# A decayed linear-attention stage inside a three-part kernel: order of two scans, one copy of the state, place of the small VectorE operations

## The chip, the core and the metric

One NeuronCore of a Trainium2 chip runs the whole program. The metric is the time of one execution in microseconds, as the median of several runs. A profile of one execution goes with it: its engines are PE (TensorE matmul) with PEld (its weight loads), DVE (VectorE), ACT (ScalarE), POOL (GpSimd) and SP (SyncE, which issues DMAs here).

## The reference

Three computations follow each other: an attention with a decaying state, a mixture of experts that picks one of eight experts for each token, and a dense maxout block. The change lies in the first, and in the part of the second that sorts tokens to experts while the first still runs.

```
B, H, S, D = 4, 8, 768, 48
for t in range(S):
    cur = einsum('bhd,bhe->bhde', u * k[t], v[t])
    y[t] = einsum('bhd,bhde->bhe', r[t], state + cur)
    state = w[t][..., None] * state + einsum('bhd,bhe->bhde', k[t], v[t])
x = y as 3072 tokens of 384
expert_idx = argmax(normalised x @ normalised emb.T / tau);  gate = softmax value of it
out[mask_e] = gate * (relu(x[mask_e] @ w1[e]) @ w2[e])
h = max(out @ a, out @ b, out @ c);  result = h @ w_out
```

## The kernel before

**Chunks.** The 768 steps of each of four batches are cut into six chunks of 128, so there are 24 chunks; chunk `g` has place `c = g % 6` in its batch. Heads go in pairs: head `2p` lies on partitions 0 to 47, head `2p+1` on partitions 64 to 111, and a tile of four pairs has 112 partitions. For each chunk two scans along time give cumulated decays: `gs` from the end backwards, `es` from the start forwards (it needs one value of `gs` per pair, through the reciprocal into `dE`). The keys times `gs` are `kS`, the receptances times `es` are `rt`. `gram` multiplies them into scores in two banks `A` (one per head of a pair), `causal` copies the scores below the diagonal into `AT`, whose diagonal POOL wrote before. `outputs` adds the state's product (`shat` with `rt`) and the product of `AT` with the values in bank `Y`; `tokens` turns the result into token rows. `kback`, `update` and `carry` bring the state to the next chunk. In `carry`, POOL multiplies the new state with the next chunk's decays twice: into `shat`, a block-diagonal copy that `outputs` uses as weights of 112 by 112, and into `Sm`, the copy that the next `carry` adds to.

**Order.** The order of instructions is written by hand in a loop over `i` from -2 to 23; each engine takes its instructions in that order. In iteration `i` the kernel handles `carry(i)`, `outputs(i)` and `tokens(i)`; `gram`, `kback`, `causal` and `update` of `g = i+1`; the bonus terms and the diagonal of `j = i+2`; the transposes, scans and products of `h = i+3`. So `rt` and `kS` made in one iteration are used by `gram` two iterations later. On PE an iteration is: `gram(g)`, transposes of w, `kback`, bonus sum, transposes of k, `outputs(i)`, bonus turn, transposes of r, `update`, `tokens(i)`. `kback` and `update` are left out for a batch's last chunk, the state's product for its first.

**Banks.** The transposes of w, k and r go around two banks `T`: w of the next chunk needs the bank that k of this chunk was in, which is free when `kS` is made. Six users go around three banks `M`, `tokens` and `update` among them; `logits` (`dot`) and `carry` (`S`) on DVE set them free. At the start `transpose` of w for chunk 1 takes the bank `T` in which the k of chunk 0 lies.

**Routing.** Sets of three chunks (two at the end) are routed while attention goes on. `route_expert` gives five small DVE operations, in the iterations `i` = 3, 6, 9 and so on; `route_rank` counts ranks on PE and `route_slot` gives twelve small DVE operations in `i` = 4, 7, 10, 13, 16, 19. They are put in a list, `fillers`. `fill()` issues the next one from the list; it stands between the larger DVE operations (after each masked copy, after each scan, after `kS`), and `fill(99)` issues what is left at the end of the iteration.

Of the kernel before, what the change touches and what calls it, by code (L numbers as in the profile page):

```python
# [7 lines left out]
F32 = mybir.dt.float32  # L8
F32R = mybir.dt.float32r
BF16 = mybir.dt.bfloat16  # L10
# [29 lines left out]
NOWHERE = 100000  # L40

# [5 lines left out]
class Block:  # L47
# [64 lines left out]
    def attention(self):  # L112
# [3 lines left out]
        with ExitStack() as es:  # L116
# [44 lines left out]
            shat = [cp.tile([112, NP, 112], F32, name=f"shat{i}") for i in range(2)]  # L161
# [11 lines left out]
            cum = cp.tile([P, E], BF16, name="cum")  # L173
# [59 lines left out]
            def setup2b():  # L233
# [6 lines left out]
                for q, o in ((0, 0), (1, 64)):  # L240
                    act.activation(out=sel[o:o + D, :, q * D:(q + 1) * D],
                                   in_=ident[o:o + D, o:o + D].unsqueeze(1).to_broadcast([D, NP, D]), func=AF.Copy)
                act.activation(out=sel[:, :, 96:104], in_=tp[:112, :32].rearrange("q (p e) -> q p e", p=NP), func=AF.Copy)
                act.activation(out=flat(self.enT), in_=tq[:, :24], func=AF.Copy)

            def setup4():
                pool.memset(one1, 1.0)
                for k in range(E):
                    for i in range(2):
                        pool.memset(caprow[:, i, k:k + 1], float(CAPS[i][k]))  # L250
                for t, m, base in ((w7, -1, E - 1), (pos, 1, 0)):
                    pool.iota(t, pattern=[[m, E]], base=base, channel_multiplier=0, allow_small_or_imprecise_dtypes=True)

            def setup3():
                for t in yT + shat:
                    pool.memset(t, 0.0)
                pool.memset(acc, 0.0)
                pool.memset(cum, 0.0)
                pool.memset(oneb, 1.0)
                pool.affine_select(out=tri, in_=oneb, pattern=[[1, P]], compare_op=ALU.is_gt, fill=0.0,  # L260
                                   base=0, channel_multiplier=-1)
                for t, pat, base, mul in ((w8, [[-1, E]], E, 0), (i128, [[1, P]], 0, 0),
                                          (i32, [[1, 32]], -32, 0), (tid, [[P, NG]], 0, 1)):
# [5 lines left out]
            def transpose(g, which):  # L269
# [3 lines left out]
                t = bank("T", 2)  # L273
# [45 lines left out]
            def scan(g):  # L319
# [9 lines left out]
                x["kS"] = wp.tile([112, 512], F32, tag="kS", name="kS", bufs=3)  # L329
                scaled = lambda: dve.tensor_tensor(out=x["kS"].rearrange("q (p t) -> q p t", p=NP),  # L330
                                                   in0=x["k"][:112].rearrange("q (p t) -> q p t", p=NP),
                                                   in1=gs[:, :, 1:], op=ALU.mult)
                if g > 0:
                    scaled()
                fill()
# [4 lines left out]
                if g == 0:  # L340
                    scaled()
# [45 lines left out]
            def carry(g):  # L387
# [9 lines left out]
                j = (g + 1) % 2  # L397
                decay = lambda o, n: pend[o:o + n, g + 1, :].unsqueeze(2).to_broadcast([n, NP, D])
# [43 lines left out]
            def fill(n=1):  # L442
# [7 lines left out]
            def route_expert(g0, n):  # L450

                sl = slice(g0, g0 + n)
                r = rt_[g0] = {}
                b8 = lambda z: z.unsqueeze(2).to_broadcast([P, n, E])
                w8b = w8.unsqueeze(1).to_broadcast([P, n, E])
                m, e8, r["mx"], r["oh"] = (small("m", [P, n]), small("e8", [P, n, E]), small("mx", [P, n]),
                                           small("oh", [P, n, E], BF16))
                ops = [lambda: dve.tensor_reduce(out=m, in_=dot[:, sl, :], axis=X, op=ALU.max)]
                if n == 1:
                    ops += [lambda: dve.scalar_tensor_tensor(out=e8[:, 0], in0=dot[:, g0, :], scalar=m, in1=w8,  # L460
                                                             op0=ALU.is_equal, op1=ALU.mult)]
                else:
                    ops += [lambda: dve.tensor_tensor(out=e8, in0=dot[:, sl, :], in1=b8(m), op=ALU.is_equal),
                            lambda: dve.tensor_tensor(out=e8, in0=e8, in1=w8b, op=ALU.mult)]
                ops += [lambda: dve.tensor_reduce(out=r["mx"], in_=e8, axis=X, op=ALU.max),
                        lambda: dve.tensor_tensor(out=r["oh"], in0=w8b, in1=b8(r["mx"]), op=ALU.is_equal)]
# [814 lines left out]
```

## Time and profile before

| | |
|---|---|
| median of 3 runs | 737.52 us (733.77 to 738.44) |
| the profiled execution | 733.96 us, span 732.2 us, mean granted clock 0.992 |
| attention loop | from about 13 to 187 us of the span |
| PE, DVE, POOL busy | 708.7, 428.2, 257.0 us |

The span is what the profile covers. The attention loop takes the first quarter; the experts follow up to about 419 us and the dense block up to about 711 us.

### The profile page before, as it was taken

To read this page: it belongs to the slowest core of one execution; us is meant where nothing else is said; L and a number is where in the kernel's file an instruction comes from. 1 tells how busy PE (TensorE), PEld (TensorE's weight loads), DVE (VectorE), ACT (ScalarE), POOL (GpSimd) and SP (SyncE) were. 2 spreads that over 40 slices of the span, in tenths; PEclk is the share of its full clock that TensorE was granted. 3 is DMA by queue.
4 is the path that set the end of the run, shared out by engine and by line. 5 is a ranking of instruction groups with operands and counts; after the bars stand their busy time and mean duration, and the time that the engine had idled before them with its cause. 6 is when DMAs were issued, how large, how long until landed. Compare 5 with 4: busy or idle time off the path is not lost.

```text
span 732.2 us, 13468 instructions
## 1 busy us (share of the span) xinstructions
PE 708.7 (97%) x4861; PEld 627.6 (86%) x4861; DVE 428.2 (58%) x938; ACT 306.8 (42%) x720; POOL 257.0 (35%) x271
## 2 busy tenths in 40 slices
PE   7999999999799999999999999999999999999994
PEld 4788888888789999999999988988988988889884
DVE  7889999998747986878788368431032031221110
ACT  4667666765445554555556322222121221221120
POOL 6857657476531401201100023343333333223122
PEclk9999999999999999999999999999999999999998
DMA  9997878753365537656554111000100100000001
GB/s 154 171 149 139 138 135 138 144 89 118 104 186 165 170 115 216 202 152 195 152 173 147 60 29 59 23 22 1 44 1 0 44 1 11 33 1 21 22 2 46
DMA packets 146444, 69.05 MB, mean 94 GB/s; under 512 B 104967, under 2 KB 140931, under 8 KB 146360
## 3 DMA queue, kind: packets, MB, share of 16 engines
q1 hardware_dynamic: 141752, 58.27, 35.1%
q0 software_dynamic: 4032, 9.74, 4.2%
q8 instruction: 42, 0.69, 0.4%
q14 instruction: 42, 0.34, 0.1%
q10 hardware_dynamic: 576, 0.01, 0.1%
HBM read 58.52 MB, written 9.48 MB: 93 GB/s over the span
## 4 chain that ended last, share of the span: by engine, by line
PE 85%; DVE 7%; issue 3%; DMA 2%; ACT 1%; POOL 1%; SPq 0%; POOLq 0%; DVEq 0%; ACTq 0%
PE psy L993 16%; PE psT L993 15%; PE psy L933 13%; PE psh L916 13%; PE psh L1017 9%; PE psT L275 4%; PE psA L356 3%; PE psM L426 3%; PE psY L417 3%; PE psY L410 2%; PE psM L384 1%; DMA out_dram<-raw,idx 1%; DVE es L337 1%; PE psM L294 1%; DVE gs L324 1%
## 5 line engine op out<-in xcount | busy, mean ns | idle before, releaser
L999 DVE TENSOR_TENSOR xg<-psT,xg 128x512 f32<-128x512 f32 x18 | 12.4, 690 | 112.8 <-PE psT L993 80.8
L827 DVE TENSOR_TENSOR lw<-raw,hw 128x384 fp32r<-128x384 f32 x120 | 62.3, 553 | 15.8 <-ACT hw L825 14.0
L825 ACT ACTIVATE hw<-raw 128x384 fp32r<-128x384 f32 x123 | 60.7, 524 | 17.7 <-ACT hw L825 10.2
L1007 POOL TENSOR_TENSOR lw<-xg,hw 128x512 fp32r<-128x512 f32 x24 | 31.5, 1311 | 100.4 <-ACT hw L1006 100.4
L841 POOL DMA_INDIRECT xg<-xs_d,idxs x25 | 26.8, 1073 | 111.0 <-PE psT L903 44.6
L1007 POOL TENSOR_TENSOR lh<-xg,hh 128x512 fp32r<-128x512 f32 x12 | 16.1, 1340 | 115.1 <-ACT hh L1006 115.1
L309 POOL TENSOR_SCALAR_AFFINE_SELECT AT<-c 128x1024 f32<-128x1024 f32 x24 | 38.9, 1619 | 49.0 <-ACT c L304 48.9
L1006 ACT ACTIVATE hw<-xg 128x512 fp32r<-128x512 f32 x24 | 15.2, 635 | 97.0 <-DVE xg L1000 97.0
L993 PE MATMUL psy<-yh,mh 128*128 128x512 f32 x162 | 46.7, 396 | 0.2 <-ACT ys L937 0.2
L993 PE MATMUL psy<-yl,mh 128*128 128x512 f32 x162 | 46.6, 395 | 0.0
L993 PE MATMUL psT<-yh,ml 128*128 128x512 f32 x162 | 46.6, 396 | 0.0
L993 PE MATMUL psy<-yh,ml 128*128 128x512 f32 x162 | 46.5, 396 | 0.0
L993 PE MATMUL psT<-yl,mh 128*128 128x512 f32 x162 | 46.5, 396 | 0.0
L993 PE MATMUL psT<-yh,mh 128*128 128x512 f32 x162 | 46.5, 395 | 0.0
L922 DVE SCALAR_TENSOR_TENSOR lh<-psh,hh 128x420 fp32r<-128x420 f32 (+6 forms) x56 | 31.4, 561 | 19.8 <-ACT hh L921 19.5
L916 PE MATMUL psh<-xh,hw 128*128 128x420 f32 (+7 forms) x177 | 42.0, 345 | 0.3 <-DVE lh L922 0.3
L916 PE MATMUL psh<-xh,lw 128*128 128x420 f32 (+7 forms) x183 | 42.0, 339 | 0.0
L1033 POOL DMA_INDIRECT out_dram<-raw,idx x24 | 23.7, 987 | 49.5 <-ACT raw L1023 32.5
L916 PE MATMUL psh<-xl,hw 128*128 128x420 f32 (+7 forms) x177 | 40.7, 337 | 0.0
L933 PE MATMUL psy<-hh,hw 128*128 128x420 f32 (+6 forms) x168 | 40.1, 344 | 0.0
L933 PE MATMUL psy<-lh,hw 128*128 128x420 f32 (+6 forms) x168 | 39.2, 341 | 0.0
L933 PE MATMUL psy<-hh,lw 128*128 128x420 f32 (+6 forms) x168 | 39.2, 341 | 0.0
(329 smaller groups left out, 1801.7 us busy)
## 6 DMA issues: line engine op xcount, KB each, us to landing
raw<-in_moe_w_dram SPq DMA_DIRECT2D x128, 192.0 KB
raw<-in_moe_w_dram SPq DMA_DIRECT2D x18, 384.0 KB
wb<-in_w_dram SPq DMA_DIRECT2D x24, 192.0 KB
kb<-in_k_dram SPq DMA_DIRECT2D x24, 192.0 KB
rb<-in_r_dram SPq DMA_DIRECT2D x24, 192.0 KB
vb<-in_v_dram SPq DMA_DIRECT2D x24, 192.0 KB
xs_d<-xt SPq DMA_DIRECT2D x24, 192.0 KB
raw<-in_moe_w_out_dram SPq DMA_DIRECT2D x6, 384.0 KB
```

The costliest lines, as they stand in the source:

```text
L275: pe.transpose(t[:112, p * P:(p + 1) * P], flat(src)[:, p * P:p * P + 112], ident)
L309: pool.affine_select(out=x["AT"].rearrange("s q p t -> s (q p) t"), in_=x["c"].rearrange("t q p -> t (q p)").unsqueeze(2).to_broadcast([P, ...
L825: self.act.activation(out=hi, in_=raw, func=AF.Copy)
L827: eng.tensor_tensor(out=lo, in0=raw, in1=hi.bitcast(F32), op=ALU.subtract)
L841: self.pool.indirect_dma_start(out=t[:n], out_offset=None, in_=self.xs_d[0:rows], in_offset=bass.IndirectOffsetOnAxis(ap=self.idxs[:n, 4 * ...
L916: self.pe.matmul(t[:, c0:cap], a[:, d, :], b[:, d, c0:], start=(n == 0), stop=(n == 8))
L922: self.dve.scalar_tensor_tensor(out=lo, in0=t[:, c0:cap], scalar=0.0, in1=hi.bitcast(F32), op0=ALU.max, op1=ALU.subtract)
L933: self.pe.matmul(self.yb[m][:, :cap], a[:, m, :], b, start=(f == 0 and n == 0), stop=(f == 7 and n == 2))
L993: self.pe.matmul(t, a[:, d, f * P:(f + 1) * P], b[:, d, :], start=(n == 0), stop=(n == 8))
L1007: self.pool.tensor_tensor(out=lo, in0=c2, in1=hi.bitcast(F32), op=ALU.subtract)
L1017: self.pe.matmul(t[:, :DM], a[:, c], b[:, f, :], start=(n == 0), stop=(n == 17))
L1033: self.pool.indirect_dma_start(out=self.out, out_offset=bass.IndirectOffsetOnAxis(ap=self.idx2[:, k:k + 1], axis=0), in_=o, in_offset=None ...
```

## The change

The state is kept once: POOL writes one tile `held` of 112 by 192, which is the weights of the state's product and the summand of the next `carry`. The state's product is written as eight products of 48 rows instead of four of 112. Both scans stand ahead of `kS` and `rt` for every chunk. In the loop up to `i` = 19 the small operations all stand behind the two masked copies; from `i` = 20 on `fill()` works as before. Transposes of w for chunk 1 take a bank `A`. Ranks are counted with wider products (nine become four for a set of three), in doubled numbers; the counting of a set is one reduction into the next set's tile instead of three additions; the list's slot needs one operation less, and `aa` has one tensor operand instead of two. Some constants are made by other small instructions.

```
-            shat = [cp.tile([112, NP, 112], F32, name=f"shat{i}") for i in range(2)]
+            held = [cp.tile([112, NP * D + 16], F32, name=f"held{i}") for i in range(2)]
...
+                dve.tensor_scalar(out=i32, in0=i32, scalar1=HALF + 0.5, scalar2=None, op0=ALU.add)
...
-                t = bank("T", 2)
+                t = bank("A" if (g, which) == (1, "w") else "T", 2)
...
                 fill()
-                x["kS"] = wp.tile([112, 512], F32, tag="kS", name="kS", bufs=3)
-                scaled = lambda: dve.tensor_tensor(out=x["kS"]..., in1=gs[:, :, 1:], op=ALU.mult)
-                if g > 0:
-                    scaled()
-                fill()
                 dve.tensor_tensor_scan(out=flat(es_), data0=wz[j][:, :-1], data1=flat(dE), ...)
                 x["es"] = es_
-                if g == 0:
-                    scaled()
+                fill()
+                x["kS"] = wp.tile([112, 512], F32, tag="kS", name="kS", bufs=3)
+                dve.tensor_tensor(out=x["kS"]..., in1=gs[:, :, 1:], op=ALU.mult)
                 fill()
...
-                for o in (0, 64):
-                    pool.tensor_tensor(out=shat[j][o:o + D, :, o:o + D], in0=sn[o:o + D], in1=decay(o, D), op=ALU.mult)
-                if c < CH - 2:
-                    state[b] = wp.tile([112, NP, D], F32, tag="Sm", name="Sm", bufs=1)
-                    pool.tensor_tensor(out=state[b], in0=sn, in1=decay(0, 112), op=ALU.mult)
+                hold = state[b] = held[(g + 1) % 2][:, :NP * D].rearrange("q (p e) -> q p e", p=NP)
+                pool.tensor_tensor(out=hold, in0=sn, in1=pend[:, g + 1, :].unsqueeze(2).to_broadcast([112, NP, D]),
+                                   op=ALU.mult)
...
                     for p in range(NP):
-                        pe.matmul(t[:112, p * P:(p + 1) * P], shat[j][:, p, :], x["rt"][:, p * P:(p + 1) * P],
-                                  start=(p == 0), stop=False)
+                        for o, m in ((0, 64), (64, D)):
+                            pe.matmul(t[o:o + m, p * P:(p + 1) * P], held[j][o:o + D, p * D:p * D + m],
+                                      x["rt"][o:o + D, p * P:(p + 1) * P], start=(p == 0), stop=False)
...
-            def fill(n=1):
+            def fill(n=None):
+                if n is None:
+                    n = len(spread)
...
-                for i in range(n):
-                    o = rk[:, i * E:(i + 1) * E]
-                    pe.matmul(o, oneb, cum, start=True, stop=False)
-                    for k in range(i):
-                        pe.matmul(o, oneb, r["oh"][:, k, :], start=False, stop=False)
-                    pe.matmul(o, tri, r["oh"][:, i, :], start=False, stop=True)
+                pe.matmul(o, twob, r["cum"].unsqueeze(1).to_broadcast([P, n, E]), start=True, stop=False)
+                for k in range(n - 1):
+                    pe.matmul(o[:, k + 1:], twob, r["oh"][:, k:k + 1].to_broadcast([P, n - 1 - k, E]), ...)
+                pe.matmul(o, tri, r["oh"], start=False, stop=True)
...
-                    return lambda: dve.tensor_tensor(out=cum, in0=cum, in1=r["oh"][:, i, :], op=ALU.add)
+                        dve.tensor_reduce(out=ohs[(r["set"] + 1) % 3][:, 0], in_=ohs[r["set"] % 3][:, :n + 1]..., op=ALU.add)
...
-                    lambda: dve.tensor_scalar(out=rq, in0=ri, scalar1=7, ..., op0=ALU.logical_shift_right),
-                    lambda: dve.tensor_scalar(out=rl, in0=ri, scalar1=4095 - 384, ..., op0=ALU.bitwise_and),
-                    lambda: dve.scalar_tensor_tensor(out=aa, in0=r["mx"], scalar=-4.0, in1=rq, op0=ALU.mult, op1=ALU.add),
+                    lambda: dve.tensor_scalar(out=rl, in0=ri, scalar1=1, scalar2=4095 - 384, ...),
+                    lambda: dve.tensor_scalar(out=aa, in0=ri, scalar1=2.0 ** -8, scalar2=HALF, op0=ALU.mult, op1=ALU.add),
...
+                    if i == NG - 4:
+                        spread.append(True)
...
                         causal(g)
+                    if not spread:
+                        fill(99)
...
-                    fill(99)
+                    if spread:
+                        fill(99)
```

## Rows read from the trace of the kernel before

**Rows 1.** The page: busy time by engine, and the chain that ended last.

```profile
PE 708.7 (97%) x4861; PEld 627.6 (86%) x4861; DVE 428.2 (58%) x938; ACT 306.8 (42%) x720; POOL 257.0 (35%) x271
...
PE 85%; DVE 7%; issue 3%; DMA 2%; ACT 1%; POOL 1%; SPq 0%; POOLq 0%; DVEq 0%; ACTq 0%
```

**Rows 2.** Busy time by stretch: length, PE, PEld, DVE, ACT, POOL, clock, DMA.

```profile
34.60:185.00 150.40, 148.30 (x1844) 126.66 (x1844) 136.19 (x325) 100.37 (x268) 96.92 (x115) 1.00 0.72 130
```

**Rows 3.** The chain, 85.0 to 92.3 us (i = 9): start, length, what.

```profile
85.03 1.09 PE psA L356 x16
86.12 0.58 PE psT L275 x4
...
88.02 0.88 PE psY L410 x8
88.90 1.01 PE psY L417 x16
...
90.17 0.44 PE psT L275 x4
...
91.20 1.07 PE psM L426 x8
```

**Rows 4.** DVE in order of time, i = 7: start, length, what.

```profile
70.75 0.75 DVE L362 COPY_PREDICATED AT<-msk,psA 128x512 f32<-128x512 int32 x1
...
72.69 1.22 DVE L324 TENSOR_TENSOR_SCAN gs<-wz,dG 112x516 f32<-112x516 f32 x1
...
76.16 0.69 DVE L348 TENSOR_TENSOR rt<-psT,es 112x512 f32<-112x512 f32 x1
...
77.00 1.20 DVE L505 SCALAR_TENSOR_TENSOR aa<-mx,rq 128x3 f32<-128x3 f32 x1
...
78.59 0.70 DVE L495 TENSOR_SCALAR pay<-i,aa,tid 128x32 fp32r<-128x32 f32 x3
...
79.31 0.34 DVE L396 TENSOR_TENSOR S<-Sm,psM 112x192 f32<-112x192 f32 x1
```

**Rows 5.** POOL in order of time, i = 7.

```profile
76.92 1.27 POOL L288 TENSOR_TENSOR z<-kT,rT 112x512 f32<-112x512 f32 x1
```

**Rows 6.** PE in order of time, i = 8: idle time before it and releaser in brackets.

```profile
79.54 0.43 PE L294 MATMUL psM<-z,uh 112*32 112x128 f32 x8 [0.47 <-DVE dot L437]
```

**Rows 7.** The chain, 49.0 to 55.6 us (i = 4, batch's last chunk in gram).

```profile
49.07 1.09 PE psA L356 x16
...
50.95 0.36 PE psM L294 x8
...
54.47 1.14 PE psM L426 x8
```

**Rows 8.** ACT in order of time, i = 4.

```profile
53.30 0.21 ACT L327 ACTIVATE pend<-gs 112x4 f32<-112x4 f32 x1 [0.72 <-DVE gs L324]
53.82 0.60 ACT L419 ACTIVATE yT<-psY 112x512 f32<-112x512 f32 x1 [0.31 <-PE psY L417]
```

**Rows 9.** DVE in order of time, i = 21: dependent small operations without a large one between.

```profile
174.66 0.15 DVE L500 TENSOR_TENSOR ro<-psM,oh 128x16 f32<-128x16 f32 x1
...
175.05 0.17 DVE L503 TENSOR_SCALAR rq<-ri 128x2 int32<-128x2 int32 x1
```

**Rows 10.** All engines in order of time, 8 to 18 us, chunks 0 and 1.

```profile
10.02 0.68 DVE L348 TENSOR_TENSOR rt<-psT,es 112x512 f32<-112x512 f32 x1
...
10.16 1.10 PE L275 MATMUL psT<-ident,wb 128*112 128x128 f32 x4 [2.04 <-DVE kS L330]
...
11.93 1.23 DVE L324 TENSOR_TENSOR_SCAN gs<-wz,dG 112x516 f32<-112x516 f32 x1 [1.23 <-ACT wz L277]
...
14.16 1.91 DVE L337 TENSOR_TENSOR_SCAN es<-wz,dE 112x516 f32<-112x516 f32 x1
...
14.96 2.17 POOL L288 TENSOR_TENSOR z<-kT,rT 112x512 f32<-112x512 f32 x1
...
17.19 0.42 PE L294 MATMUL psM<-z,uh 112*32 112x128 f32 x8 [1.38 <-POOL z L288]
```

More of the change, by code (lines that the diff above doesn't have):

```diff
@@ L40 @@
 NOWHERE = 100000
+HALF = 2.0 ** 23 - 0.5
 def flat(t):
@@ L172, in attention @@
             tri = cp.tile([P, P], BF16, name="tri")
-            cum = cp.tile([P, E], BF16, name="cum")
+            twob = cp.tile([P, P], BF16, name="twob")
+            ohs = [cp.tile([P, 4, E], BF16, name=f"ohs{i}") for i in range(3)]
             acc = cp.tile([P, 32], F32, name="acc")
@@ L250, in setup4 @@
                         pool.memset(caprow[:, i, k:k + 1], float(CAPS[i][k]))
-                for t, m, base in ((w7, -1, E - 1), (pos, 1, 0)):
-                    pool.iota(t, pattern=[[m, E]], base=base, channel_multiplier=0, allow_small_or_imprecise_dtypes=True)
+                pool.iota(pos, pattern=[[1, E]], base=0, channel_multiplier=0, allow_small_or_imprecise_dtypes=True)
+                dve.tensor_scalar(out=w7, in0=pos, scalar1=-32769.0, scalar2=E - 1 - 8192.0, op0=ALU.mult, op1=ALU.add)
             def setup3():
-                for t in yT + shat:
+                for t in yT + held:
                     pool.memset(t, 0.0)
                 pool.memset(acc, 0.0)
-                pool.memset(cum, 0.0)
                 pool.memset(oneb, 1.0)
-                pool.affine_select(out=tri, in_=oneb, pattern=[[1, P]], compare_op=ALU.is_gt, fill=0.0,
+                pool.memset(twob, 2.0)
+                pool.affine_select(out=tri, in_=twob, pattern=[[1, P]], compare_op=ALU.is_gt, fill=0.0,
                                    base=0, channel_multiplier=-1)
-                for t, pat, base, mul in ((w8, [[-1, E]], E, 0), (i128, [[1, P]], 0, 0),
-                                          (i32, [[1, 32]], -32, 0), (tid, [[P, NG]], 0, 1)):
+                pool.affine_select(out=tri, in_=tri, pattern=[[1, P]], compare_op=ALU.not_equal, fill=1.0,
+                                   base=0, channel_multiplier=-1)
+                for t, pat, base, mul in ((w8, [[-1, E]], E, 0), (i128, [[1, P]], 1024, 0), (ohs[0][:, 0], [[32, E]], 8, 0),
+                                          (i32, [[32, E], [1, 4]], 8, 0), (tid, [[P, NG]], 0, 1)):
                     pool.iota(t, pattern=pat, base=base, channel_multiplier=mul,
@@ L440, in attention @@
             rt_, fillers = {}, []
-            def fill(n=1):
+            spread = []
+            def fill(n=None):
+                if n is None:
+                    n = len(spread)
                 while fillers and n:
@@ L452, in route_expert @@
                 sl = slice(g0, g0 + n)
-                r = rt_[g0] = {}
+                k = len(rt_)
+                r = rt_[g0] = {"set": k}
+                r["cum"], r["oh"] = ohs[k % 3][:, 0], ohs[k % 3][:, 1:n + 1]
                 b8 = lambda z: z.unsqueeze(2).to_broadcast([P, n, E])
                 w8b = w8.unsqueeze(1).to_broadcast([P, n, E])
-                m, e8, r["mx"], r["oh"] = (small("m", [P, n]), small("e8", [P, n, E]), small("mx", [P, n]),
-                                           small("oh", [P, n, E], BF16))
+                m, e8, mx = small("m", [P, n]), small("e8", [P, n, E]), small("mx", [P, n])
                 ops = [lambda: dve.tensor_reduce(out=m, in_=dot[:, sl, :], axis=X, op=ALU.max)]
[L459 to L466, printed above, removed]
+                ops += [lambda: dve.tensor_tensor(out=e8, in0=dot[:, sl, :], in1=b8(m), op=ALU.is_equal),
+                        lambda: dve.tensor_tensor(out=e8, in0=e8, in1=w8b, op=ALU.mult),
+                        lambda: dve.tensor_reduce(out=mx, in_=e8, axis=X, op=ALU.max),
+                        lambda: dve.tensor_tensor(out=r["oh"], in0=w8b, in1=b8(mx), op=ALU.is_equal)]
                 return ops
@@ L488, in rank, with count @@
                         dve.tensor_reduce(out=ri, in_=ro, axis=X, op=ALU.add)
-                def count(i):
-                    return lambda: dve.tensor_tensor(out=cum, in0=cum, in1=r["oh"][:, i, :], op=ALU.add)
+                def count():
+                    with nc.allow_low_precision(reason="small integers"):
+                        dve.tensor_reduce(out=ohs[(r["set"] + 1) % 3][:, 0],
+                                          in_=ohs[r["set"] % 3][:, :n + 1].rearrange("p n e -> p e n"), axis=X, op=ALU.add)
                 def place(i):
@@ L496, in place @@
                                                      scalar2=tid[:, g:g + 1], op0=ALU.is_equal, op1=ALU.mult)
-                return ([count(i) for i in range(n)] if g0 + n < NG else []) + [
+                return ([count] if g0 + n < NG else []) + [
                     lambda: dve.tensor_tensor(out=ro, in0=r["rk"][:, :n * E].rearrange("q (n e) -> q n e", n=n),
@@ L543, in totals @@
                 tot = st["tot"] = bank("M", 3)
-                pe.matmul(tot[:1, :E], oneb[:, 0:1], cum, start=True, stop=False)
+                pe.matmul(tot[:1, :E], oneb[:, 0:1], rt_[g0]["cum"], start=True, stop=False)
                 for k in range(n):
@@ L564, in leader @@
                 tp = bank("T", 2)
-                pe.matmul(tp[:1, :E], oneb[:, 0:1], cum, start=True, stop=True)
+                pe.matmul(tp[:1, :E], oneb[:, 0:1], ohs[6 % 3][:, 0], start=True, stop=True)
                 return [
```

20 lines of the change are left out of this document (9 added, 11 removed).

## The prediction

> **What bounds the kernel now.** I read first the page's busy times and the chain that ended last [rows 1]: PE is busy 97% of the span and makes 85% of the chain, DVE 7%. So what an edit gives on DVE, ACT or POOL counts only where PE waits for it. Then busy time by stretch: in the attention loop's steady part, 34.6 to 185 us, PE is busy 148.30 of 150.40 us [rows 2]. It idles 2.1 us in all, and that is four waits of about half a microsecond (i = 8, 14, 20, 21), of which the first stands in [rows 6]. In the chain of an undisturbed iteration [rows 3] every step is a PE step; the iteration is as long as PE's instructions. The experts and the dense block behind the loop are PE's as well and not touched, so the sum is how much earlier or later the attention loop ends.
>
> One thing must be seen before costing DVE: `rt` and `kS` of an iteration are used by `gram` two iterations later. A later `rt` does not hold up the next `gram`. What holds PE up from DVE is a bank that is released late, or an ACT step queued behind a late scan.
>
> **A. The state's product.** Before, four products of 128 columns take 0.88 us, 0.22 each at line L410 [rows 3]. After, eight products, each 48 rows to half of the output partitions. The trace of before has no product that is halved both ways; the nearest rows are the eight products of `AT` with the values, halved by output partitions, 1.01 us for eight of 128 columns, and `gram`, halved by input rows, 1.09 us [rows 3]. Both show that two halves overlap: one after the other, eight at 0.22 would be 1.76. I also read a price for a change of form: the same four transposes take 0.58 us right behind `gram` and 0.44 behind another transpose [rows 3], and the new product follows transposes of full size and precedes the products with the values, so it pays that. I take 1.01, the nearest row: +0.13 us. Bounds: nothing (0.88; a gain is excluded because as many columns stream through each half as before) to 1.76 (+0.88). There are 20 chunks with a state; in three of them PE waits anyway (D), so 17 × 0.13 = **+2.2 us**, bounds 0 to +17.6.
>
> The halves of the new product write into one bank, at different partitions, while those of `gram` write into two banks. The Trainium skill, TensorEngine Tiling (Array Packing), section Restrictions and Gotchas, says: "Different row tiles cannot access same PSUM bank simultaneously". No row here shows such a case; by that rule the halves would come one after the other, which is the upper bound just given, and the sum would be some 15 us higher. It is the first rival below.
>
> **B. Ranks.** Nine products take 0.21 us: from the end of the transposes at 49.07 + 1.09 + 0.58 = 50.74 to 50.95 [rows 3, 7]. Four take about 0.1. Six sets in the loop, three of them in iterations of D: 3 × 0.11 = **-0.3 us**.
>
> **C. Small operations off the place behind `rt`.** In iteration 7, `rt` ends at 76.85, and then the rest of the list runs until `S` at 79.31 [rows 4]: 2.4 us, of which `aa` alone is 1.20, because it ends with POOL's `z` at 78.19 [rows 4, 5]. `S` releases a bank `M`, and PE waits 0.47 us for that [rows 6] (the trace names `dot`, the operation just before `S`). After, nothing stands between `rt` and `dot`, and the counting, in a tile of its own, needs no wait for PE. Then `rt` ends 8.0 us behind the begin of `gram` (1.2 to the copies, 1.3 for them, 1.8 for the small operations, see D, and 3.7 for scans and products: 72.69 to 76.85 less the small operations between [rows 4]) and `S` 0.4 later; PE wants the bank 9.5 us behind it, at 79.07 [rows 6]. Of the four waits one is at i = 21, behind the leader's small operations, which stay where they were; but DVE comes to them some 1.5 us earlier, so that it goes as well. **-2.1 us**; bounds -2.1 to -1.5 (the last stays).
>
> **D. What the small operations delay instead.** All of a set's operations now stand ahead of `gs`. Their length, n = 3: counting 0.1, two dependent steps 0.39 [rows 9], `rl` and `aa` 0.2, `ohb` 0.4 (78.20 to 78.59), `pay` 0.6 [rows 4]: about 1.8 us. On ACT the copy `pend` waits for `gs`, and queued behind it are `yT`, the turn of the bonus terms, `rT` and `xt`; `tokens` on PE waits for `yT`. In iteration 4, which has no `kback` and `update` to fill the time, `gram` begins at 49.07 and `tokens` at 54.47 [rows 7], `pend` at 53.30 and `yT` at 53.82 [rows 8]. After: copies from 49.07 + 1.2, two of them 1.3, small operations 1.8, `gs` 1.22 [rows 4], so `pend` at 54.6, `yT` 0.21 later, done 0.60 later at 55.4: `tokens` about 0.85 us late. Three iterations are like that (4, 10, 16): **+2.5 us**. In the others of the kind (7, 13, 19) `kback` and `update` put `tokens` 6.2 us behind the begin of `gram` [rows 3], and `yT` is ready 6.3 behind it: 0. Bounds: 0 (DVE ahead of time) to +5 (all six, by way of POOL, whose diagonal and `z` come later too, and PE's bonus sum waits for `z`).
>
> **E. The start.** PE's transposes of w for chunk 1 waited 2.04 us for the bank that `kS` of chunk 0 held, ended at 11.3, and `gs` of chunk 1 began at 11.93 [rows 10]. In a bank `A` they can run at 8.2, if the load is there; then DVE is free for `gs` when `rt` of chunk 0 ends, 10.70, plus 0.1 for an added operation: 1.1 us earlier. Next, `es` of chunk 1 ran 14.16 to 16.07, 1.91 us against the 1.22 of a scan of its size [rows 4, 10], beside `z`, which took 2.17 against 1.27 alone [rows 5, 10]; PE then idled 1.38 us for `z` [rows 10]. After, `es` follows `gs`: 10.8 + 1.25 + 0.2 + 1.23 = 13.5, and most of `z` runs without it, done near 14.9 instead of 17.13. So PE's bonus sum comes 2.3 us earlier; for chunk 2 the same clash is loosened a little more. **-2.5 us**, bounds -1.1 (the bank alone) to -4 (both waits for `z` gone).
>
> **At no cost or gain.** POOL multiplies once instead of three times; the result is wanted an iteration later, and POOL is idle a good part of each iteration. The order of `es` and `kS` in the steady part: `kS` comes 1.2 us later, still well before w's transposes want its bank. DMAs are issued as before.
>
> **Sum.** 2.2 - 0.3 - 2.1 + 2.5 - 2.5 = -0.2 us. The profiled execution took 733.96, so it becomes 733.8; the median of the runs shown is 3.6 above that execution, so **737.3 us** is the forecast.
>
> **Rivals.** First, **the halves do not overlap** because they share a bank: the product takes 1.76, 20 × 0.88 = 17.6 instead of 2.2, and the time is 737.3 + 15.4 = 752.7 us, slower. For it: no row has two input halves in one bank. Against it: halves by output partitions do overlap within one bank, and these halves differ in output partitions as well. It makes the change slower from a product of about 1.4 us on: 7.4 us, 1%, over 20 chunks is 0.37 above 1.01. Chance 0.12.
>
> Second, **the costs stay out**: the product takes 0.88 and `yT` is never late. Then -2.2 and -2.5 more, 732.6; with the start's full 4 us, 731.1. For it: 1.01 and 0.85 are worked out, not seen. Against it: the price of a change of form is in every step of the chain. Chance 0.15.
>
> Third, **the delay reaches all six sets**, through `yT` and `z`, and the start gives only its bank: +2.5 and +1.4, 741.2 us. For it: in the sets of iterations 7, 13 and 19 the cover is within 0.1 us. Chance 0.15. That the four waits do not go (DVE is late for another reason) would be 739.4 and lies inside the forecast's range.
>
> **How the numbers follow.** The forecast has 0.58. About 1%, 7.4 us, is what a measurement of this kernel tells from no change; before's own runs spread over 4.7 us. Faster by more than that needs the second rival with the start's bound and more: 0.06. Slower is the first rival and a little of the third: 0.14. The rest, 0.80, is no change. The range 731 to 743 holds the second and third rivals and leaves out the first with some of the spread.
>
> **What would show it.** Right: the state's product takes 1.0 us in the chain, no PE wait for `dot` after i = 7, `gs` of chunk 1 near 10.8, a wait of `tokens` for `yT` in i = 4, 10, 16, the steady part as long as before to within 2 us. Wrong: a product near 1.7 us, which decides the sign; `tokens` that waits in none or all of the six sets; `gs` of chunk 1 still at 12 because its load was late.

## The result and the profile after

The changed kernel took **744.78 us** (median of 8 runs, 740.96 to 751.08), the kernel before 736.89 beside it (8 runs, 733.57 to 738.53). The ratio is 1.0117, 95% interval 1.0079 to 1.0155: slower by 1.2%, outside the forecast's range, on the side that had 0.14. The profiled execution took 744.58, its span 742.9, 10.7 more than before.

The page after: busy time by engine, and the chain that ended last.

```profile
PE 715.7 (96%) x4984; PEld 631.0 (85%) x4985; DVE 423.4 (57%) x917; ACT 305.3 (41%) x720; POOL 218.2 (29%) x236
...
PE 88%; DVE 5%; issue 2%; DMA 2%; POOL 1%; ACT 1%; POOLq 0%; SPq 0%; ACTq 0%; DVEq 0%
```

The chain of iteration 9 after, to hold against [rows 3]: start, length, what.

```profile
85.32 1.09 PE psA L357 x16
86.41 0.58 PE psT L280 x4
...
88.31 1.01 PE psY L409 x15
89.32 1.01 PE psY L416 x16
```

The state's product takes 1.01 us, as forecast; its halves overlap within one bank. The next view is PE in order of time after, with the idle time before an instruction in brackets.

```profile
10.52 0.42 PE L299 MATMUL psM<-z,uh 112*32 112x128 f32 x8 [1.48 <-POOL z L293]
...
49.84 0.43 PE L299 MATMUL psM<-z,uh 112*32 112x128 f32 x8 [0.16 <-DVE dot L436]
...
54.93 1.14 PE L425 MATMUL psM<-sel,yT 112*128 112x104 f32 x8 [1.36 <-ACT yT L418]
...
98.97 1.14 PE L425 MATMUL psM<-sel,yT 112*128 112x104 f32 x8 [0.85 <-ACT yT L418]
...
143.00 1.14 PE L425 MATMUL psM<-sel,yT 112*128 112x104 f32 x8 [0.85 <-ACT yT L418]
...
189.66 0.17 PE L477 MATMUL psM<-ohs,twob 128*128 128x8 bf16 x1 [6.57 <-DVE fl L536]
```

The four waits for `dot`, of which [rows 6] shows the first, are gone, and one of 0.16 us has come in i = 4. The three waits of `tokens` for `yT` have come, in i = 4, 10 and 16. The last line nobody had forecast. Here are POOL and DVE ahead of it, in order of time, at the end of the loop (i = 22). There POOL issues a gather (`DMA_INDIRECT`, a DMA that fetches rows by index). Behind it stand seven POOL operations of 128x384 that compute the low part of the first expert's weights (`raw` less its high part); below they are called the row.

```profile
180.65 0.51 POOL L399 TENSOR_TENSOR held<-S,pend 112x192 f32<-112x192 f32 x1 [1.21 <-PE psA L357]
...
181.38 1.07 POOL L849 DMA_INDIRECT hw<-xs_d,idxs  x1 [0.22 <-issue]
...
182.01 7.18 DVE L464 TENSOR_TENSOR e<-e,w 128x16 f32<-128x16 f32 x1
182.47 1.01 POOL L835 TENSOR_TENSOR lw<-raw,lw 128x384 fp32r<-128x384 f32 x1
...
183.43 2.89 POOL L835 TENSOR_TENSOR lw<-raw,hw 128x384 fp32r<-128x384 f32 x3
...
186.28 2.88 POOL L835 TENSOR_TENSOR oh<-raw,oh 128x384 fp32r<-128x384 f32 x3
189.23 0.17 DVE L465 TENSOR_REDUCE mx<-e 128x2 f32<-128x16 f32 x1
```

A product of 128x16 (`e`, a step of the routing) takes 7.18 us. It ends as POOL's row ends (186.28 + 2.88), which follows POOL's gather at once. The same place in the kernel before, POOL and DVE in order of time:

```profile
180.63 0.16 DVE L464 TENSOR_TENSOR e<-e,w 128x16 f32<-128x16 f32 x1
180.86 0.51 POOL L400 TENSOR_TENSOR shat<-S,pend 48x192 f32<-48x192 f32 x1 [1.08 <-DMA hw<-xs_d,idxs]
181.64 1.07 POOL L841 DMA_INDIRECT hw<-xs_d,idxs  x1 [0.28 <-POOL shat L400]
182.78 1.02 POOL L827 TENSOR_TENSOR lw<-raw,lw 128x384 fp32r<-128x384 f32 x1
183.76 3.09 POOL L827 TENSOR_TENSOR lw<-raw,hw 128x384 fp32r<-128x384 f32 x3
184.19 0.85 DVE L507 TENSOR_TENSOR ohb<-i,rl 128x256 fp32r<-128x256 f32 x1 [1.26 <-PE psM L515]
184.97 1.92 DVE L495 TENSOR_SCALAR pay<-i,aa,tid 128x32 fp32r<-128x32 f32 x2
```

Here `e` took 0.16 us, ahead of the gather. The DVE operations that fell into the row waited for about one of its operations each (`ohb` 0.85, two `pay` 1.92). What the long wait does further is in the windows: before, then after, the columns as in [rows 2].

```profile
185.00:205.00 20.00, 15.58 (x113) 13.41 (x111) 12.68 (x50) 7.44 (x21) 7.74 (x8) 0.91 0.44 132
```

```profile
185.00:205.00 20.00, 15.34 (x97) 14.28 (x97) 11.62 (x43) 5.68 (x16) 5.17 (x6) 0.57 0.19 61
```

After PE's 6.57 us of idling the mean granted clock of the stretch is 0.57: PE ran much of it at 1.2 in place of 2.4 GHz, and the last products of the state (L409) took 1.97 us.

Where the 10.7 us came from, by the begin of `gram` in PE's order of time and the experts' first product (`psh`):

| | before | after | difference |
|---|---|---|---|
| gram of chunk 1 | 19.36 | 19.25 | -0.1 |
| gram of chunk 2 | 27.22 | 25.71 | -1.5 |
| gram of chunk 23 | 178.04 | 179.42 | +1.4 |
| first `psh` | 203.84 | 214.90 | +11.1 |

In these two executions the start gives 1.5, the loop from chunk 2 on costs 2.9, and the 25 us behind the loop cost **9.7**.

### The profile page after: what moved, and what is told of

Its sections match the earlier page's. It is cut to its first block, busy times and chain, and to the rows that moved or that the text cites. A ratio compares the mean times of both kernels' runs of the same rounds, so it can differ in the third digit from the quotient of the medians.

```text
span 742.9 us, 13674 instructions
## 1 busy us (share of the span) xinstructions
PE 715.7 (96%) x4984; PEld 631.0 (85%) x4985; DVE 423.4 (57%) x917; ACT 305.3 (41%) x720; POOL 218.2 (29%) x236
## 4 chain that ended last, share of the span: by engine, by line
PE 88%; DVE 5%; issue 2%; DMA 2%; POOL 1%; ACT 1%; POOLq 0%; SPq 0%; ACTq 0%; DVEq 0%
PE psy L1001 15%; PE psT L1001 14%; PE psy L941 13%; PE psh L924 13%; PE psh L1025 8%; PE psT L280 4%; PE psM L425 4%; PE psA L357 4%; PE psY L416 2%; PE psY L409 2%; PE psM L385 1%; DVE AT L363 1%; PE psT L911 1%; DMA out_dram<-raw,idx 1%; DVE e L464 1%
## 5 line engine op out<-in xcount | busy, mean ns | idle before, releaser
L314 POOL TENSOR_SCALAR_AFFINE_SELECT AT<-c 128x1024 f32<-128x1024 f32 x24 | 30.7, 1281 | 90.4 <-ACT c L309 90.4
```

The costliest lines, as they stand in the source:

```text
L314: pool.affine_select(out=x["AT"].rearrange("s q p t -> s (q p) t"), in_=x["c"].rearrange("t q p -> t (q p)").unsqueeze(2).to_broadcast([P, ...
```

## The experiments

The theories to begin with: **P**, the loss is the meeting of DVE's small operations with POOL's row in the tail (the stretch behind the loop); **L**, it is the change's longer loop and start, and the long `e` is harmless. Ratios below are to the kernel before, run beside the experiment on the same chip, with 95% intervals; the edits are shown shortened.

**One part, or the place of the operations.** e1 issues the expert's choice ahead of the last masked copies; e2 delays DVE there in the kernel before; e3 is the kernel before with the state kept once; e4 the changed kernel with the small operations spread from the first iteration on.

```
e1:  +   if i == NG - 2: fill(4)              # ahead of causal(g)
e2:  +   if i == NG - 2: 3 x dve.memset(dE)   # ahead of causal(g)
e3:  before, shat[2] and Sm -> held, eight products
e4:  -   spread = []            +   spread = [True]
```

> The changed kernel with one edit: in iteration 22 the four remaining operations that pick the experts of chunks 20 and 21 stand ahead of the masked copies instead of between and behind them. Theory P (POOL starves one DVE operation): the multiplication of e with w, which took 7.18 us at 182.0 beside POOL's gather and seven multiplications in a row, now runs at about 181.0, before the gather at 181.4, and takes about 0.2; PE's wait of 6.57 us goes, and the half clock behind it with it; the kernel ends 8 to 11 us sooner, 734 to 737 us, and the attention loop before it (gram of chunk 23 at 179.4) stays where it is. Theory L (the loop with its longer product and later scans makes the loss, and the 7 us are only the place where the lateness shows): at most 1 to 2 us sooner, 743 us.

> The kernel before with one edit: three fills of a tile that is no longer needed (about 0.5 us each) stand on DVE ahead of the masked copies of iteration 22, so that the same multiplication is issued about 1.5 us later, at 182.1 instead of 180.6, inside POOL's gather (181.6 to 182.7) and ahead of its row of multiplications. Theory P: it is starved as in the changed kernel, 6 to 8 us long, PE waits 5 us or more, the kernel takes 8 to 11 us more than before, 744 to 748 us. Theory L: 1 to 1.5 us more, 738 us.

> The kernel before with one part of the change: the state kept once, with the eight products. Theory P: the product takes 1.01 instead of 0.88 us in 20 chunks, so the loop ends 2 to 2.6 us later (gram of chunk 23 at 180.1 to 180.7), while POOL's gather comes when its indices are there; the multiplication of e with w is then starved or not as its place against the gather has it, 739 us if not, 747 if it is, and nothing between. Theory L: 739 to 740 us, with no long operation on DVE.

> The changed kernel with one part undone: the small operations are issued one at a time between the large ones all through the loop, as in the kernel before. Then tokens waits for yT in iterations 4, 10 and 16 no longer (2.5 us sooner by term D of the prediction) and DVE is late for PE again in iterations 8, 14, 20 (some 1 to 1.5 us lost): gram of chunk 23 about 1 us sooner than in the changed kernel, at 178.4. Theory P: whether the multiplication is starved hangs on 1 us here; 744 us if it is, 734 if not. Theory L: 743 to 744 us.

Measured: e1 738.85 us, 1.0062 [1.0035, 1.0089]; e2 738.48, 1.0033 [1.0009, 1.0057]; e3 **745.23**, 1.0144 [1.0110, 1.0179]; e4 741.89, 1.0104 [1.0069, 1.0139]. In e1 `e` is early (0.37 us), but then `rl`, a later step of the routing, takes 5.50 us to the end of the row. In e3 `e` takes 7.18, in e4 `oh` 6.96. From the `gram` of chunk 23 to the first `psh` e3 takes 35.6 us, as the changed kernel (35.5) and not as the kernel before (25.8). In e2, though delayed, no operation waits longer than about one of POOL's. So the state kept once is enough to bring the loss, and P missed on e2: lateness on DVE alone doesn't do it.

**Whose work it is.** e6 puts the seven remainders on DVE behind its small operations, e7 does the same to the kernel before. e5 and e13 leave the row on POOL: e5 makes POOL later, e13 puts a small memset between gather and row.

```
e6, e7:  -   eng = self.pool if n == 1 and e == 0 else self.dve
         +   dve, the first three behind the second fill(99)
e5:      +   3 x pool.memset(dE)              # ahead of self.gather(0, PRE, 1)
e13:     +   pool.memset(dE[:, :, 0:1], 0.0)  # behind it
```

> The changed kernel with three memsets of an unused tile on POOL ahead of its last gather of the loop (i == NG-2), so that the gather and the row of seven split multiplications start about 1.5 us later (a memset of that size took 0.52 us in setup). Nothing else. Theory P (the loss is the meeting of DVE's `e` with POOL's gather and row): `e` takes under 0.4 us, the wait of 6.57 us on PE for DVE at 189.66 is gone, later DVE operations in the row wait one POOL operation at a time as before, and the time falls to 736 to 740 although work was added. Theory L (the loss comes from the change's own longer loop and start): 743 to 747, `e` moved or not.

> The changed kernel with the remainders of expert 0's first weights (seven operations lw/hw/oh <- raw) on DVE, behind its small operations, in place of POOL; ScalarE's copies stay where they are. POOL then has only the gather there. Theory P: no small operation of DVE takes over 1.2 us in 180 to 192 us, PE's wait of 6.57 us is gone, 735 to 739. Theory L: 743 to 747.

> The kernel before with the same move of the seven remainders to DVE. In the kernel before `ohb` and the two `pay` waited about one POOL operation each (2.8 us in place of 0.9), while seven remainders on DVE are about 3.5 us in a stretch where DVE idled about as long. Theory P: 734 to 737.5, and the changed kernel with the same move lies within 3 us of it, against 7.9 us between the two kernels as they are. Theory L: the two stay 6 to 9 us apart.

> The changed kernel with one memset of 112x4 on POOL (about 0.1 us) between its last gather of the loop and the row of seven split multiplications; nothing else. Theory S (a row that follows the gather directly isn't left by POOL between its operations, and anything in between ends that): no operation of DVE in 181 to 190 us takes over 1.3 us, PE's wait of 6.57 us for DVE is gone, 736 to 740. Theory T (it is the moment at which DVE's operation comes, not what stands between): `e` or the next operation with two inputs takes 6 to 8 us still, 743 to 747.

Measured: e5 742.33, 1.0112 [1.0077, 1.0147]; e6 **739.03**, 1.0064 [1.0036, 1.0092]; e7 736.24, 1.0030 [1.0003, 1.0058]; e13 745.83, 1.0142 [1.0111, 1.0172]. With no row on POOL the two kernels are 2.8 us apart in place of 7.9: theory P holds for the rest, L falls. But e5 shows that it isn't a matter of a moment: there `e` ran in time, and the operation that came next to the row, `rl`, took 8.22 us.

**The meeting by itself.** Three kernels (e9, e14, e16) carry trials ahead of everything, on tiles of their own: a row of seven 128x384 operations on POOL, and on DVE memsets that set the moment (one `dve.memset` each), a 128x16 product of two inputs in SBUF, a reduction and a second product. Their times aren't compared.

```
pool.indirect_dma_start(got <- 128 rows)            # in some kinds
for i in range(7): pool.tensor_tensor(y[i], x[i], x[(i + 1) % 7], subtract)
for _ in range(m): dve.memset(pad, 0.0)
dve.tensor_tensor(c, a, b, mult); dve.tensor_reduce(d, c); dve.tensor_tensor(c, a, d, mult)
```

> The changed kernel with a measurement ahead of it, on tiles of its own: 22 trials, each a row of seven multiplications' kind on POOL (128x384, two inputs in SBUF) that begins together with DVE, and on DVE a number of memsets (none to 16, to shift the moment), then a 128x16 product with two inputs in SBUF, a reduction, and a second product. In the last 12 trials a gather stands ahead of POOL's row. The run's own time is not compared. Theory Q (DVE waits for the one POOL operation that runs): every product takes under 1.3 us, wherever it falls. Theory R (a row without gaps can keep DVE out to its end): some products take as long as what is left of the row (3 to 7 us), and if only those that come at the row's first operation do, the trials show it by the moment.

e9 in order of time: a trial without a gather (its row runs from 13.87), then one with it.

```profile
13.84 0.11 DVE L136 TENSOR_TENSOR mc<-ma,mb 128x16 f32<-128x16 f32 x1
13.87 2.89 POOL L133 TENSOR_TENSOR my<-mx,mx 128x384 f32<-128x384 f32 x3 [0.27 <-DVE mx L128]
...
14.19 0.69 DVE L138 TENSOR_TENSOR mc<-ma,md 128x16 f32<-128x16 f32 x1
...
92.63 0.96 POOL L130 DMA_INDIRECT mgot<-in_moe_w_dram,miz  x1 [0.33 <-DVE mpad L135]
93.32 7.00 DVE L136 TENSOR_TENSOR mc<-ma,mb 128x16 f32<-128x16 f32 x1
93.60 6.68 POOL L133 TENSOR_TENSOR my<-mx,mx 128x384 f32<-128x384 f32 x7
```

Without a gather all 20 products took 0.11 to 0.79 us, wherever they fell: at most what was left of one operation of POOL (DVE is let in). Behind a gather, in 12 of 12 trials one product ended with the row (DVE is kept out): 7.55 down to 4.00 us, by the moment. The moment sets only how much of the row is left. But the kernel before has a gather ahead of its row too.

> The changed kernel with a second measurement ahead of it: 21 trials of a gather, a row of seven on POOL and a 128x16 product on DVE, in seven kinds of three: the row directly behind the gather; a 128x384 product of POOL ahead of the gather, which the gather waits for; a memset of 128x4 between gather and row; a copy of 128x4 between; a row whose first operation waits for DVE until the gather is over; a row whose operations wait for one another; a copy that waits for the gathered rows between. The run's own time is not compared. The directly following row keeps DVE out for what is left of it (4 to 7 us). Theory S: the kinds with something between, or with a wait, let DVE in at the next boundary (under 1.3 us); the kind with the product ahead tells whether the gather's own wait is what let DVE in in the kernel before. Theory T: all kinds keep DVE out alike.

e14 in order of time: one trial with a memset between, one with a row whose operations wait for one another.

```profile
71.03 0.97 POOL L133 DMA_INDIRECT mgot<-in_moe_w_dram,miz  x1 [0.74 <-DVE mpad L150]
72.00 0.12 POOL L137 MEMSET mtiny<- 128x4 f32 x1
72.06 6.69 POOL L147 TENSOR_TENSOR my<-mx,mx 128x384 f32<-128x384 f32 x7
73.19 5.59 DVE L151 TENSOR_TENSOR mc<-ma,mb 128x16 f32<-128x16 f32 x1
...
146.85 0.96 POOL L133 DMA_INDIRECT mgot<-in_moe_w_dram,miz  x1
147.84 1.00 POOL L147 TENSOR_TENSOR my<-mx,mx 128x384 f32<-128x384 f32 x1
148.92 6.35 POOL L147 TENSOR_TENSOR my<-mx,my 128x384 f32<-128x384 f32 x6
149.28 0.66 DVE L151 TENSOR_TENSOR mc<-ma,mb 128x16 f32<-128x16 f32 x1
```

Row directly behind, product ahead, memset between, copy between: 12 of 12 kept out (4.57 to 8.04 us). A chain in the row, or a copy that waits for the gathered rows: none of 6 kept out (at most 0.91; in one of them both products fell ahead of the row). A late first operand: two let in; in the other trial the operand was there before the gather ended, POOL had nothing to wait for, and the product took 6.83. So neither "anything in between" nor the moment holds; it is whether **POOL waits** between the gather and the row, or in it.

> The changed kernel with a third measurement ahead of it: 12 trials of a gather, a row of seven on POOL and a 128x16 product on DVE, in four kinds of three: two 48x192 products of POOL ahead of the gather, the second waiting for the first (as in the kernel before), operations of the row without waits; the same with a load and a copy of ScalarE that each operation of the row waits for, long done; one 112x192 product ahead (as in the changed kernel), with the loads and copies; no product, with the loads and copies. The run's own time is not compared. If what stands ahead of the gather decides, the two kinds with two products let DVE in at each boundary (under 1.3 us) and the others keep it out for what is left of the row; if it is something else in the kernel before, all 12 keep it out.

e16 in order of time: two products ahead of the gather, the second waiting for the first (as in the kernel before), then one (as in the changed kernel).

```profile
55.42 1.24 POOL L139 TENSOR_TENSOR mgot<-ms,ms 48x192 f32<-48x192 f32 x2 [3.54 <-DVE miz L136]
56.94 0.99 POOL L143 DMA_INDIRECT mgot<-in_moe_w_dram,miz  x1 [0.27 <-POOL mgot L139]
57.99 6.71 POOL L146 TENSOR_TENSOR my<-mx,mh 128x384 f32<-128x384 f32 x7
58.25 0.76 DVE L149 TENSOR_TENSOR mc<-ma,mb 128x16 f32<-128x16 f32 x1
...
92.99 0.59 POOL L142 TENSOR_TENSOR mgot<-ms,ms 112x192 f32<-112x192 f32 x1 [3.50 <-DVE miz L136]
93.85 0.99 POOL L143 DMA_INDIRECT mgot<-in_moe_w_dram,miz  x1 [0.27 <-POOL mgot L142]
94.86 6.69 POOL L146 TENSOR_TENSOR my<-mx,mh 128x384 f32<-128x384 f32 x7
95.82 5.77 DVE L149 TENSOR_TENSOR mc<-ma,mb 128x16 f32<-128x16 f32 x1
```

Two products ahead: no product of 6 trials over 0.77 us. One or none: 4.07 to 6.81 in 6 of 6. In the kernel before the second product waited besides for the rows of an earlier gather (1.08 us); the pair here has no such wait, and DVE is let in all the same. There is a mark to read in this run: from the end of the gather to the row it is 0.06 or 0.07 us where DVE is let in (57.93 to 57.99), 0.01 to 0.03 where it isn't (94.84 to 94.86). In the kernel before it is 182.71 to 182.78, in the changed one 182.45 to 182.47. The mark doesn't hold for a row with a wait of its own: in the chain of e14 the distance is 0.03 (147.81 to 147.84), and DVE is let in.

**The wait in the changed kernel.** e15 adds a copy to e13 that reads what the memset wrote; e17 only gives POOL as many instructions as before.

```
e15:  +   pool.memset(dE[:, :, 0:1], 0.0)                 # behind self.gather(0, PRE, 1)
      +   pool.tensor_copy(dE[:, :, 1:2], dE[:, :, 0:1])
e17:  +   memsets of big on POOL in place of the products saved
```

> The changed kernel with two small operations of POOL (112x4 each) between its last gather of the loop and the row of seven: a memset, and a copy that reads what the memset wrote, so that POOL waits once for itself. The memset alone changed nothing. Theory W (behind a gather POOL's operations are let through without a break until POOL has waited once for something): no operation of DVE in 181 to 190 us takes over 1.3 us (they wait for one operation of POOL at most), PE's wait of 6.57 us is gone, 736 to 740. If a wait of POOL on itself isn't what decides: 743 to 747.

> The changed kernel with memsets of 32x112 on POOL (about 0.18 us) in place of the products that it saves, so that POOL's instructions have the same places in its stream as in the kernel before; the gather and the row follow each other as in the changed kernel, one memset ahead of the gather. If the place in POOL's stream decides whether the row is left between operations: DVE gets in, 736 to 740. If the operations themselves and their waits decide: `e` or its neighbour takes 6 to 8 us, 743 to 747.

Measured: e15 **734.80**, 1.0003 [0.9981, 1.0025]; e17 745.64, 1.0160 [1.0123, 1.0197], `e` 7.27 us. POOL and DVE of e15 in order of time:

```profile
182.79 1.07 POOL L851 DMA_INDIRECT hw<-xs_d,idxs  x1 [0.23 <-issue]
183.43 0.15 DVE L464 TENSOR_TENSOR e<-e,w 128x16 f32<-128x16 f32 x1
...
183.86 0.13 POOL L631 MEMSET dE<- 112x4 f32 x1
...
184.06 0.19 POOL L632 COPY dE<-dE 112x4 f32<-112x4 f32 x1
...
184.22 0.99 POOL L837 TENSOR_TENSOR lw<-raw,lw 128x384 fp32r<-128x384 f32 x1
...
185.15 1.04 DVE L509 TENSOR_SCALAR aa<-ri 128x2 f32<-128x2 int32 x1
```

`e` starts 0.43 us ahead of the gather's end, where it also starts in the changed kernel (0.44); there it takes 7.18, here 0.15. The memset alone (e13) changed nothing, so it is the wait: two operations of 112x4 on POOL, of which the second waits for the first, take back the whole loss.

**The rest of the change.** e8: the kernel before with the new start alone. e11, e12: the state alone, and the small operations and ranks alone, both with the remainders on DVE, to be held against e7. e10 puts the two copies of the state back, spreads the small operations in i = 4, 10, 16 and makes `w7` on POOL; e18 is e15 with these last two.

```
e10, e18:  +   spread[:] = [True] if i % 6 == 4 or i >= NG - 4 else []
           +   pool.tensor_scalar(out=w7, in0=pos, ...)
```

> The kernel before with only the order of the start and scans: the second chunk's decays in a bank of the scores, and the second scan ahead of the keys' product. By the prediction's step for the start (2.5 us off) 733.5 to 734.5; by the trace of the changed kernel (1.5 us off at the second chunk's scores, under a half clock) 735 to 736; if the lower clock takes all of it back, 736 to 738. No operation of the tail is touched, so that `e` should run ahead of POOL's gather as in the kernel before.

> The kernel before with the state kept once (eight products of the two halves) and nothing else of the change, the seven remainders on DVE, so that POOL has no row there. Beside e7 (the kernel before with the remainders on DVE). If the prediction's price holds (17 x 0.13 us) 2.2 us above it: 737 to 739.5. If POOL's shorter work gives some back, 0 to 1 us above. The 9 us that this part brought with the row on POOL are gone either way by the theory of the meeting; by its rival the time stays at 743 to 747.

> The changed kernel without the state kept once and without the new start (both as in the kernel before), the seven remainders on DVE: what is left are the small operations, fewer and behind the masked copies, and the ranks' products. By the prediction's steps minus 0.3, minus 2.1, plus 2.5: 0 beside e7; with the waits for `yT` as the changed kernel's trace has them (3.1 us) 0.7 above: 735 to 738.

> The changed kernel with three things put back: the two scaled copies of the state with four products (so POOL's two products stand ahead of the gather again), the small operations spread one by one in every sixth step (i = 4, 10, 16), and the row w7 made on POOL. Kept: the start, both scans first, the small operations behind the masked copies in the other steps. By the rows of the changed kernel: the four waits on `dot` (2.1 us) and the start (1.5 us) are won, the state's product (2.2 us), the waits for `yT` (3.1 us) and the meeting in the tail (7 us) are gone: about 3 us below the kernel before, 731 to 735. Rival: `e` meets POOL's row all the same, or the start's gain is taken back by the clock: 736 to 744.

> The changed kernel with POOL's wait on itself behind the gather (as e15), the small operations spread one by one again in every sixth step (i = 4, 10, 16) and the row w7 made on POOL. If the three waits of PE for `yT` (1.36, 0.85 and 0.85 us in the changed kernel) are gone and nothing comes in their place, about 3 us below e15: 730 to 733, some 0.4% below the kernel before. Rival: the spread operations delay the scans or bring back waits for `dot` (as with the operations spread in every step): 733 to 736, no difference.

Measured: e8 733.76, 0.9984 [0.9961, 1.0007]; e11 740.57, 1.0069 [1.0046, 1.0092]; e12 743.74, 1.0106 [1.0074, 1.0137]; e10 734.43, 0.9996 [0.9970, 1.0022]; e18 733.21, **0.9970** [0.9942, 0.9998]. The kernel before took 735.95 beside e11 and e12 and 733.87 beside e7, so they are compared by their ratios: e11 is 0.39% above e7, about 2.9 us, and e12 0.76%, about 5.6 us, each with some 3 us of uncertainty. e12 was expected at most 0.7 above e7 and missed by about 5. From chunk 2 to chunk 23 the `gram`s of its profiled execution, the slowest of its six, take 156.7 us, 5.9 over the kernel before. The steps behind i = 4, 10 and 16 are longer by 2.3, 0.9 and 0.9, eight others by 0.2 or 0.3, and one by 1.5, with the granted clock at 0.57 (60 to 64 us) after a wait of 1.51 us in i = 4; the steps to chunks 10, 16, 22 and 23 are shorter by 0.3 to 0.6. The changed kernel has +2.9 there, with the state's dearer product in it. So with the old order of the scans the lump of small operations cost more, and the parts don't add up one by one. e10's and e18's spread took the three waits for `yT` away; shorter ones, of 0.2 to 0.4 us, came in other steps. e18 is the only kernel below the one before by an interval that leaves out 1; it does so barely, and as one of fifteen such intervals that can be chance.

## Why the prediction was wrong

**The step that failed** is "At no cost or gain. POOL multiplies once instead of three times". It counted instructions and looked where their result is wanted; it didn't ask what POOL does next with DVE beside it. In iteration 22 the second `shat` of the kernel before (180.86) is followed by the gather and the row of seven, and with that pair of products ahead DVE got in between the row's operations. With one product, DVE waits 7 us, PE 6.57, and PE goes on for a while at half its clock: 9.7 us behind the loop, for which the sum had nothing. e3 brings the loss with this edit alone, e15 takes it away with one wait, e17 shows that it isn't the number of instructions. In the seven profiled kernels with one product, the row on POOL and no added wait (the changed one, e1, e3, e4, e5, e13, e17) a DVE operation was kept out to the row's end; in the four with the pair (the one before, e2, e8, e10) none was.

**The terms of the sum**, by the trace after:

- **A**, the product: 1.01 us, right; the steps of e11's loop that have this product and no wait are 0.13 to 0.15 longer. From chunk 2 to 23 e11 takes 152.55 against 150.82: +1.7, forecast +2.2. The first rival (no overlap in one bank) fell. It was the Trainium skill's rule in TensorEngine Tiling (Array Packing), section Restrictions and Gotchas; the product of 1.01 in place of 1.76 doesn't bear it out for halves that also differ in output partitions.
- **C**, the four waits: right. The steps to the `gram`s of chunks 10, 16, 22 and 23 went from 8.02, 8.03, 8.12, 6.78 to 7.63, 7.62, 7.72, 6.01: 2.0 together, with A's 0.13 in them.
- **D**: the right three iterations, and the small operations take 1.82 us in i = 4 (51.11 to 52.93), as forecast. That two of the waits are 0.85 to the hundredth is luck: the prediction's own steps (`yT` done at 55.4, `tokens` at 54.47) add up to 0.93. The first took 1.36, because the new `w7` on DVE waited 1.63 us for POOL's `pos`, queued behind sixteen small memsets; together 3.06, forecast 2.5. The move of `w7` to another queue had not been priced. Seven kernels were profiled with this longer wait, and in two of them it cost more: in e15 the granted clock after it is 0.57 from 56 to 60 us, and the next step takes 9.16 in place of 7.62; in e5 the clock is 0.68 there. The changed kernel's profiled run kept 1.00.
- **E**, the start: `gs` of chunk 1 at 10.58 (forecast 10.8), and `z` took 1.27 without `es` beside it. But 2.5 us became 1.5 at chunk 2, and 0.1 at chunk 1: the granted clock of the first 20 us was 0.83 against 0.91, after PE had idled 1.48 us for `z`, and the first `gram` took 2.08 us. One execution of each tells little here, for with one and the same start the `gram` of chunk 2 begins anywhere within 2 to 3 us: at 25.72 to 28.52 in the six kernels profiled with the old start (27.0 in the mean), at 24.81 to 26.85 in the eleven with the new one (25.8). That is a gain of 1.2 us, half of the forecast. Alone (e8) the start gave 0.16%, 1.2 us too, with no change inside the interval.
- **B** wasn't measured by itself.

From chunk 2 to chunk 23 the loop came out 2.9 longer where A to D add up to 2.3, and with the start in it the `gram` of chunk 23 is within 1.6 us of the forecast's -0.2. e15, at 1.0003, has the number that was forecast, but not its terms, and that is luck: in its profiled execution the `gram` of chunk 2 is 1.6 us earlier than before, the loop 4.4 longer (1.5 of it by the clock) and the tail 2.2 shorter (23.6 us in place of 25.8). With the remainders on DVE the two kernels are 2.8 us apart.

**Still open**: why a wait of POOL on itself ahead of the gather (the second of two products) works as one behind it, while the gather's own wait for a single product doesn't; and why a wait behind the gather also frees an `e` that begins 0.43 us ahead of the gather's end, and so ahead of that wait (e15). The runs show when DVE is kept out, not by what.

## What to carry to other kernels

Before taking an instruction off an engine with slack, look at what follows it there: beside a row of operations that compete with another engine it may have been the pause that let the other one in. Where small DVE operations feed PE beside a long row on POOL, read whether they wait for one operation or for the row; a single dependent operation on POOL can decide that, and putting the row elsewhere removes the question. Here edits that are each worth a third of a percent were decided by such a meeting rather than by their own sum.

## What the runs showed of the hardware that wasn't expected

POOL's operations behind an indirect gather keep DVE's operations with two SBUF inputs (and `tensor_scalar` on int32) out until the whole row is over (up to 8.22 us, `rl` in e5), as long as POOL has not waited for anything between the gather and the row or in it; after a wait, DVE gets in at the next boundary (about 1 us at most). Two products ahead of the gather, the second waiting for the first, let DVE in as well (6 of 6 trials). Reductions and operations that read PSUM ran beside the row at their usual 0.17 us (in e1, before `rl` was kept out).

The Trainium skill, SBUF — State Buffer, section Who interferes with whom, says that a DVE operation with two SBUF inputs contends with a GpSimd operation that reads SBUF, and that the ports they share are locked for one of them at a time; where it gives a length, it is the whole instruction. The 20 products without a gather agree (0.79 at most); the 7.55 us behind a gather, over seven instructions, go beyond it.
